# Reshaping the SBUF and DRAM transfers of a two-block attention kernel: relay of spare channels only, softmax sums by two SBUF transfers and a shuffle, output rows kept in place

## The chip, the cores and the metric

The kernel runs on one core of one Trainium2 chip. The metric is device time in microseconds (us), lower is better. All profiles are of one execution on that core. Most executions of one kernel agree within about 1%; an execution over 1.5% above the fastest of the same kernel is called slow.

## The reference, cut to what matters

Two independent attention blocks, A and B, work on 2048 tokens of width 640 (32 heads of 20 channels), in bf16. Their outputs stand side by side.

```python
def _A_ref(x, wqkv, wo):            # causal window of 256 tokens, softmax
    q, k, v = ...                   # x @ wqkv, 32 heads of 20
    scores = q k^T * 20**-0.5, masked to the window
    o = softmax(scores) v
    return o @ wo

def _B_ref(x, wqkv, wo):            # linear attention
    pq, pk = phi(q), phi(k)
    num = pq (pk^T v);  den = pq . sum(pk) + 1e-6
    return (num / den) @ wo
return concatenate([A, B], axis=-1)
```

The change touches block A alone, but both blocks share the engines.

## The kernel before

A planner inside the program orders all instructions at build time, from assumed durations; on the chip every engine then runs its own list strictly in order. SyncE ("SP") issues nearly all transfers, also in order.

Q and K of block A lie in tiles of 128 partitions: four heads ("a head group") of 32 rows each. A head has only 20 channels, so the last 12 rows of each of the first five tiles hold spare channels, from which the heads of tiles 5 to 7 are put together. That relay goes through DRAM. Attention weights times V give a tile ON per group (20 rows of values and one row of softmax sums per head); there are 16 groups, 8 for each half of the tokens.

```python
# relay of Q and K: all 128 rows out, then three tiles back (twice)
def relay_write(m, tt, key):
    dst = DQK[tt][0 : 32 * NH, :].rearrange("(r b) n -> b r n", b=NH)[4 * m : 4 * m + 4, :, :]
    dma("SP", ... q.dma_start(out=dst, in_=QK[m][:, c0 : c0 + RW]) ...)          # 4 x 32 x 2048
def relay_read(g, tt, key):
    src = bass.AP(..., ap=[[NH * RW, 4], [RW, 32], [1, RW]])                      # 4 x 32 x 2048
    dma("SP", ... q.dma_start(out=QK[g][:, c0 : c0 + RW], in_=src) ...)
# ... cut ...
# sums of one head group: four hops through DRAM, the last a broadcast of 512 KB
    dma("SP", ... out=d1[:], in_=ON[nb][Dh : Dh + 97 : 32, :] ...)                # 4 x 1024 f32
    dma("SP", ... out=RC[nb][:], in_=d1[:].rearrange("a (b c) -> (a b) c", c=32) ...)
    nc.vector.reciprocal(out=RD[nb][:], in_=RC[nb][:])
    dma("SP", ... out=d2[:].rearrange("a (b c) -> (a b) c", c=32), in_=RD[nb][:] ...)
    dma("SP", ... out=RB[nb][:], in_=d2[:, None, :].to_broadcast([4, 32, TQ]) ...)
    for rg in range(2):                                                            # normalise
        nc.vector.tensor_tensor(out=os_[:, c], in0=ON[nb][:, c], in1=RB[nb][:, c], op=ALU.mult)
    dma("SP", ... out=dst, in_=os_[:] ...)                                         # rows out, 256 KB
# ... cut ...
def o_read(tt, key, earliest=0.0):                                                 # rows back
    for m in range(KT):
        src = DO[tt][:].rearrange("(r b) n -> b r n", b=32)[4 * m : 4 * m + 4, :, :]
        dma("SP", ... out=OT[:, m, :], in_=src ...)                                # 256 KB
```

The softmax here doesn't subtract the row's maximum and nothing guards it: scores larger than these inputs give would overflow.

## Time and profile before

| | before |
|---|---|
| median of three runs | 470.98 us |
| span of the profiled execution | 470.0 us |
| busy: TensorE, VectorE, ScalarE, GpSimd | 305.6, 221.4, 191.5, 128.8 us |
| mean granted TensorE clock | 0.783 |
| moved by DMA | 50.32 MB |

The page of the kernel before. The first line gives each engine's busy time (PE is TensorE, DVE VectorE, ACT ScalarE, POOL GpSimd). The next lines cut the span into 40 slices, each digit the busy share in tenths; PEclk is the clock that TensorE was granted. Then come the bytes moved, and the chain of work that ended last, by line.

```profile
PE 305.6 (65%) x5000; PEld 166.6 (35%) x5000; DVE 221.4 (47%) x442; ACT 191.5 (41%) x168; POOL 128.8 (27%) x155
...
PE   5499964650577769559784759019576938859065
...
DVE  7155522540576652425442125028589776835024
...
PEclk9589977595697978779799766658858869988558
...
DMA packets 67756, 50.32 MB, mean 107 GB/s; under 512 B 52122, under 2 KB 58906, under 8 KB 67706
...
DMA RB<-d 22%; DMA RC<-d 8%; DMA d<-RD 8%; SPq L355 7%; DMA d<-ON 6%; PE F L657 3%; PE F L622 3%; PE F L424 3%; DVE OS L602 3%; DMA OT<-do 3%; DMA do<-OS 3%; PE F L394 3%; PE F L726 2%; PE SC L483 2%; PE F L572 2%
```

No engine is full. The digits of TensorE and VectorE often fall together, which suggests that one wait stops both. The four hops of the sums (RB<-d, RC<-d, d<-RD, d<-ON) are about 43% of the chain.

The list of waits on VectorE: what waited for what, us in total, how often, longest.

```profile
DVE OS L602 <- DMA RB<-d: 97.8, 13, 21.9
DVE RD L596 <- DMA RC<-d: 36.9, 9, 10.4
DVE G L317 <- PE F L622: 21.4, 10, 17.3
```

VectorE, in order, stood 134.7 us at the sums of softmax.

The table of stretches: busy us of each engine with instruction counts, granted clock, DMA share, GB/s.

```profile
110.00:120.00 10.00, 0.00 (x0) 0.00 (x0) 0.00 (x0) 0.00 (x0) 0.00 (x0) 0.50 0.94 97
```

In such a wait nothing runs at all, and the granted clock of TensorE is one half (0.50). The chain has d<-RD from 103.7 to 113.1 us there and RB<-d from 113.1 to 121.7.

The chain that ended last, in order of time (start, us, what): a piece of the middle, then the end.

```profile
171.41 1.81 DMA RC<-d
...
173.70 4.46 DMA d<-RD
...
178.17 12.93 DMA RB<-d
...
409.49 9.87 DMA d<-ON
...
438.57 13.16 DMA OT<-do
```

The broadcast RB<-d takes 8.0 us at best, in this chain up to 14.8. But d<-ON, which carries 16 KB, takes 9.9 us too. SyncE had issued a broadcast of 512 KB at 408.88 us, 0.6 us before this hop, and by the semaphore updates in the trace the two landed together, at 419.2 and 419.4 us. So the small transfer was queueing, not moving bytes.

SyncE's instructions in order of time (start, us, instruction) show the other side of the queue.

```profile
54.49 6.63 SPq L664 DMA_DIRECT2D XT<-in_B_x_dram  x2
```

The two issues of XT kept SyncE for 6.6 us.

### The profile page before, as it was taken

What the parts mean: (1) busy time and instruction counts of PE and PEld (TensorE: products, weight loads), DVE (VectorE), ACT (ScalarE), POOL (GpSimd) and SP (SyncE); (2) the same over time, 40 slices, a digit from 0 to 9 for tenths busy, and PEclk for the clock granted to TensorE, in tenths of its full rate; (3) what the DMA queues carried; (4) which work ended last, traced back from release to release, by engine and by line L of the source; (5) the groups of instructions that cost most, each with busy time, mean ns of one, the idle gap of its engine ahead of it and who ended that gap; (6) DMA issues with size and microseconds to landing.
All of it is one profiled execution on the core that took longest, in us unless ns stands there. A gap on an engine that the chain in (4) does not pass through costs nothing.

```text
span 470.0 us, 11365 instructions
## 1 busy us (share of the span) xinstructions
PE 305.6 (65%) x5000; PEld 166.6 (35%) x5000; DVE 221.4 (47%) x442; ACT 191.5 (41%) x168; POOL 128.8 (27%) x155
## 2 busy tenths in 40 slices
PE   5499964650577769559784759019576938859065
PEld 1155432330343325235352445004233415536033
DVE  7155522540576652425442125028589776835024
ACT  1058634370174835236363325107647737410000
POOL 9004313050043413113132013203335415312002
PEclk9589977595697978779799766658858869988558
DMA  5949999298694942143449999378413423333312
GB/s 115 241 100 80 136 108 101 70 109 100 88 106 104 108 86 91 46 139 103 131 139 112 96 89 183 118 78 90 62 60 99 131 90 115 123 116 146 118 59 96
DMA packets 67756, 50.32 MB, mean 107 GB/s; under 512 B 52122, under 2 KB 58906, under 8 KB 67706
## 3 DMA queue, kind: packets, MB, share of 16 engines
q1 hardware_dynamic: 60858, 40.97, 54.2%
q0 software_dynamic: 1600, 5.34, 2.9%
q10 hardware_dynamic: 5248, 3.28, 2.7%
q8 instruction: 39, 0.64, 0.8%
q14 instruction: 11, 0.09, 0.1%
HBM read 25.30 MB, written 16.52 MB: 89 GB/s over the span
## 4 chain that ended last, share of the span: by engine, by line
DMA 53%; PE 19%; DVE 12%; SPq 10%; issue 4%; ACT 1%; POOL 0%; POOLq 0%; DVEq 0%; ACTq 0%
DMA RB<-d 22%; DMA RC<-d 8%; DMA d<-RD 8%; SPq L355 7%; DMA d<-ON 6%; PE F L657 3%; PE F L622 3%; PE F L424 3%; DVE OS L602 3%; DMA OT<-do 3%; DMA do<-OS 3%; PE F L394 3%; PE F L726 2%; PE SC L483 2%; PE F L572 2%
## 5 line engine op out<-in xcount | busy, mean ns | idle before, releaser
L490 ACT ACTIVATE P<-SC 128x2048 bf16<-128x2048 f32 x78 | 146.4, 1877 | 144.9 <-PE SC L483 143.7
L513 POOL TENSOR_TENSOR P<-P,MK 128x512 bf16<-128x512 bf16 (+1 forms) x94 | 99.7, 1068 | 276.2 <-ACT P L490 272.0
L602 DVE TENSOR_TENSOR OS<-ON,RB 128x512 bf16<-128x512 f32 x32 | 23.2, 744 | 102.0 <-DMA RB<-d 97.8
L657 PE MATMUL F<-W,X 128*128 128x320 bf16 x160 | 30.5, 343 | 41.1 <-DVE R L317 36.8
L726 PE MATMUL F<-X,XT 128*128 128x512 bf16 x100 | 28.5, 424 | 27.4 <-DVE R L317 24.1
L572 PE MATMUL F<-P,V 64*32 64x64 bf16 (+4 forms) x2144 | 31.8, 254 | 21.2 <-issue 13.1
L622 PE MATMUL F<-W,OT 128*128 128x320 bf16 x160 | 30.1, 340 | 22.6 <-DMA OT<-do 16.0
L483 PE MATMUL SC<-QK 20*64 20x128 bf16 (+4 forms) x1600 | 36.6, 272 | 4.8 <-ACT P L490 3.1
L572 PEld LDWEIGHTS <-V 64*32 64x32 bf16 x2144 | 25.5, 101 | 33.8 <-issue 33.3
L657 PEld LDWEIGHTS <-X 128*128 128x128 bf16 x160 | 16.2, 108 | 52.5 <-issue 44.1
L317 DVE CAST R<-F 128x320 bf16<-128x320 f32 (+1 forms) x55 | 28.2, 521 | 13.1 <-PE F L622 5.6
L394 PE MATMUL F<-X,WK 128*128 128x512 bf16 x75 | 25.0, 466 | 8.1 <-DVE G L317 4.8
L317 DVE CAST QK<-F 128x512 bf16<-128x512 f32 x31 | 21.1, 683 | 18.5 <-PE F L394 18.3
L394 PE MATMUL F<-X,WQ 128*128 128x512 bf16 x75 | 23.3, 429 | 9.9 <-DVE V L317 4.1
L483 PEld LDWEIGHTS <-QK 20*64 20x64 bf16 x1600 | 16.2, 111 | 36.0 <-issue 35.0
L317 DVE CAST G<-F 128x320 bf16<-128x320 f32 (+2 forms) x34 | 16.2, 486 | 26.7 <-PE F L622 21.4
L622 PEld LDWEIGHTS <-OT 128*128 128x128 bf16 x160 | 16.6, 107 | 32.8 <-DMA OT<-do 17.7
L666 PE MATMUL F<-R,XT 128*128 128x320 bf16 x160 | 27.2, 321 | 1.6 <-DVE ON L317 1.6
L513 DVE TENSOR_TENSOR P<-P,MK 128x512 bf16<-128x512 bf16 (+1 forms) x54 | 25.7, 482 | 3.7 <-ACT P L490 3.4
L424 PE MATMUL F<-WV,X 128*128 128x320 bf16 x120 | 23.8, 358 | 5.6 <-DMA WV<-in_A_wqkv_dram 4.1
L648 ACT ACTIVATE E<-R 128x640 bf16<-128x640 bf16 (+1 forms) x26 | 17.4, 688 | 20.2 <-DVE R L317 20.2
L726 PEld LDWEIGHTS <-XT 128*128 128x128 bf16 x100 | 11.4, 123 | 39.9 <-issue 33.1
(85 smaller groups left out, 339.9 us busy)
## 6 DMA issues: line engine op xcount, KB each, us to landing
RB<-d SPq DMA_DIRECT2D x16, 512.0 KB
dqk<-QK SPq DMA_DIRECT2D x10, 512.0 KB
do<-OS SPq DMA_DIRECT2D x16, 256.0 KB
QK<-dqk SPq DMA_DIRECT2D x6, 512.0 KB
XT<-in_B_x_dram SPq DMA_DIRECT2D x5, 512.0 KB
OT<-do SPq DMA_DIRECT2D x10, 256.0 KB
out_dram<-ST POOLq DMA_DIRECT2D x12, 160.0 KB, 2.7
out_dram<-G POOLq DMA_DIRECT2D x10, 160.0 KB, 2.9
```

The source lines that it names most:

```text
L317: nc.vector.tensor_copy(out=dst, in_=src)
L355: q.dma_start_transpose(out=X[slot][:, c, :], in_=xsrc[which][t * NX : (t + 1) * NX, c, :])
L394: mms.append((mm_t(NX), xkey(slot, k) + [("wqk", i, 0 if m == 0 else 1)], lambda ps, k=k: nc.tensor.matmul(ps[:], lhsT=WQK[i][:, k, m * P ...
L424: mms = [(mm_t(HALF), xkey(slot, k) + [("wv",)], lambda ps, k=k, hf=hf: nc.tensor.matmul(ps[:, 0:HALF], lhsT=X[slot][:, k, (kb % 4) * P : ...
L483: nc.tensor.matmul(SC[64 * rho : 64 * rho + 64, j, cc : cc + w], lhsT=QK[g][32 * j : 32 * j + Dh, kc : kc + 64], rhs=QK[g][32 * j : 32 * j ...
L490: nc.scalar.activation(out=pt[:], in_=SC[:], func=ACT.Exp, scale=scale)
L513: eng.tensor_tensor(out=pt[:, :, cc : cc + w], in0=pt[:, :, cc : cc + w], in1=MK[:, None, lo:hi].to_broadcast([P, 4, w]), op=ALU.mult)
L572: nc.tensor.matmul(FB[box[rg]][32 * j : 32 * j + 32, qc : qc + w], lhsT=V[kb % NV][64 * rho : 64 * rho + 64, HV * h : HV * h + 32], rhs=PT ...
L602: pl.op({"DVE": dve_ps(NX)}, lambda e, c=c: nc.vector.tensor_tensor(out=os_[:, c], in0=ON[nb][:, c], in1=RB[nb][:, c], op=ALU.mult), -2900 ...
L622: mms = [(mm_t(HALF), [lkeys(c)] if not isinstance(lkeys(c), list) else lkeys(c), lambda ps, c=c, hf=hf: nc.tensor.matmul(ps[:, 0:HALF], l ...
L657: mms = [(mm_t(HALF), [("x", slot, k), ("w1",)], lambda ps, k=k, b=b, hf=hf: nc.tensor.matmul(ps[:, 0:HALF], lhsT=X[slot][:, k, b * P : (b ...
L726: mms = [(mm_t(NX), [("x", slot, k)] + XK, lambda ps, k=k, c=c: nc.tensor.matmul(ps[:], lhsT=XW[:, k, :].rearrange("p (f c) -> p c f", c=K ...
```

## The change

The intent is that the large transfers run on 12 to 16 DMA engines and not on few. Four things change, and two assumed latencies of the planner.

1. Relay: only the 12 spare rows of a head are written, one transfer per head; the reads become one plain 128-row transfer.
2. Sums: two SBUF-to-SBUF hops of 16 KB. The second leaves one row of reciprocals in each group of 32 partitions, and a VectorE shuffle spreads it over the 32.
3. Rows: groups 0 to 4 are normalised straight into their final tile; only groups 5 to 7 go through DRAM, and they are read back into the spare rows of the five final tiles.
4. Order: groups 5 to 7 come before 3 and 4, so that the last reads are few.

```diff
+    GO = [[0, 1, 2, 5, 6, 7, 3, 4], [0, 1, 2, 5, 6, 7, 3, 4]]
-    def dma(eng, fn, mb, key, r=(), w=(), lat=2.2, ...
+    def dma(eng, fn, mb, key, r=(), w=(), lat=2.8, ...
     # relay
-        dst = DQK[tt][0 : 32 * NH, :].rearrange("(r b) n -> b r n", b=NH)[4 * m : 4 * m + 4, :, :]
-        dma("SP", lambda q: q.dma_start(out=dst, in_=QK[m][:, c0 : c0 + RW]), ...)
+        for j in range(4):
+            dma("SP", lambda q, j=j: q.dma_start(out=DQK[:, 4 * m + j, :], in_=QK[m][32 * j + Dh : 32 * j + 32, c0 : c0 + RW]), ...)
-        src = bass.AP(tensor=b.tensor, offset=b.offset, ap=[[NH * RW, 4], [RW, 32], [1, RW]])
+        src = DQK[4 * (g - KT) : 4 * (g - KT) + 4, :, :].rearrange("i d n -> (i d) n")
     # sums
-        (four transfers through d1 and d2)
+        dma("SP", lambda q: q.dma_start(out=RC[nb][:], in_=ON[nb][Dh : Dh + 97 : 32, :]), ...)
         reciprocal RD <- RC
+        dma("SP", lambda q: q.dma_start(out=RB[0:97:32, :], in_=RD[nb][:]), ...)
+            nc.vector.stream_shuffle(out=RB[:, c], in_=RB[:, c], mask=[0] * 32)
     # rows
+        if g >= KT: dst = OS        # spare groups, through DRAM
+        elif tt == 0: dst = OT[:, g, :]
+        else: dst = QK[g][:, 0:TQ]
     # ... cut: o_read in three pieces of 12-row transfers, RB set to 1.0 once ...
```

More of the change, by code (lines that the diff above doesn't have):

```diff
@@ L259 @@
     ON = [T([P, TQ], f"ON{i}", F32) for i in range(2)]
-    RB = [T([P, TQ], "RB", F32)] * 2
+    RB = T([P, TQ], "RB", F32)
     OT = T([P, KT, TQ], "OT")
-    OS = [T([P, TQ], f"OS{i}") for i in range(2)]
+    OS = T([P, TQ], "OS")
     ST = [T([P, D], f"ST{i}") for i in range(2)]
@@ L292 @@
         nc.gpsimd.memset(V[i][:], 1.0)
+    nc.gpsimd.memset(RB[:], 1.0)
     nc.gpsimd.memset(blk4[:], 1.0)
@@ L306, in qe, with dma @@
         return nc.sync if e == "SP" else nc.scalar if e == "ACTQ" else nc.gpsimd
-    def dma(eng, fn, mb, key, r=(), w=(), lat=2.2, n=1, earliest=0.0, tag=""):
+    def dma(eng, fn, mb, key, r=(), w=(), lat=2.8, n=1, earliest=0.0, tag=""):
         return pl.op({eng: (1.0 if eng == "POOL" else 0.6) * n}, lambda e: fn(qe(e)), key, r, w, lat=lat + 5.0 * mb, earliest=earliest, tag=tag)
@@ L355, in fn @@
                 q.dma_start_transpose(out=X[slot][:, c, :], in_=xsrc[which][t * NX : (t + 1) * NX, c, :])
-            pl.op({"SP": 1.3}, lambda e, fn=fn: fn(nc.sync), key, (), xkey(slot, c), lat=2.2, earliest=earliest, tag=f"x{which}{t}")
+            pl.op({"SP": 1.3}, lambda e, fn=fn: fn(nc.sync), key, (), xkey(slot, c), lat=3.0, earliest=earliest, tag=f"x{which}{t}")
     def wview(w):
@@ L400, with relay_tail @@
     RW = 4 * NX
-    DQK = [dram.tile([33 * NH, RW], BF16, name=f"dqk{i}") for i in range(2)]
-    def relay_tail(tt, key):
-        src = bass.AP(tensor=A_x.tensor, offset=A_x.offset, ap=[[RW, 12], [1, RW]])
-        dma("POOL", lambda q: q.dma_start(out=DQK[tt][32 * NH : 32 * NH + 12, :], in_=src), 0.1, key, w=[("dqk", tt)], tag="tail")
+    DQK = dram.tile([LEFT, 32, RW], BF16, name="dqk")
+    def relay_tail(key, earliest):
+        src = bass.AP(tensor=A_x.tensor, offset=A_x.offset, ap=[[LEFT * RW, LEFT], [1, LEFT * RW]])
+        dma("SP", lambda q: q.dma_start(out=DQK[:, Dh:32, :], in_=src), 0.6, key, w=[("dqkt",)], earliest=earliest, tag="tail")
     def relay_write(m, tt, key):
@@ L409, in relay_write @@
         cols = range(0, 4) if tt else range(1, 5)
-        dst = DQK[tt][0 : 32 * NH, :].rearrange("(r b) n -> b r n", b=NH)[4 * m : 4 * m + 4, :, :]
-        dma("SP", lambda q: q.dma_start(out=dst, in_=QK[m][:, c0 : c0 + RW]), 0.52, key, r=[("QK", m, z) for z in cols], w=[("dqk", tt)], tag=f"rlw{m}")
+        for j in range(4):
+            dma("SP", lambda q, j=j: q.dma_start(out=DQK[:, 4 * m + j, :], in_=QK[m][32 * j + Dh : 32 * j + 32, c0 : c0 + RW]), 0.05, key, r=[("QK", m, z) for z in cols], w=[("dqk",)], tag=f"rlw{m}")
     def relay_read(g, tt, key):
@@ L415, in relay_read @@
         cols = range(0, 4) if tt else range(1, 5)
-        o = (Dh + 4 * (g - KT)) * NH
-        b = DQK[tt][o : o + 92, :]
-        src = bass.AP(tensor=b.tensor, offset=b.offset, ap=[[NH * RW, 4], [RW, 32], [1, RW]])
-        dma("SP", lambda q: q.dma_start(out=QK[g][:, c0 : c0 + RW], in_=src), 0.52, key, r=[("dqk", tt)], w=[("QK", g, z) for z in cols], tag=f"rlr{g}")
+        src = DQK[4 * (g - KT) : 4 * (g - KT) + 4, :, :].rearrange("i d n -> (i d) n")
+        dma("SP", lambda q: q.dma_start(out=QK[g][:, c0 : c0 + RW], in_=src), 0.52, key, r=[("dqk",), ("dqkt",)], w=[("QK", g, z) for z in cols], tag=f"rlr{g}")
     def proj_v(kb, slot, key, earliest=0.0, step=0.05):
@@ L434 @@
     for tt in range(2):
-        for g in range(8):
+        for g in GO[tt]:
             for kb in (range(0, 8) if tt == 0 else range(6, 16)):
@@ L517 @@
     npv = [0]
-    DO = [dram.tile([32 * 32, TQ], BF16, name=f"do{i}") for i in range(2)]
+    DO = dram.tile([LEFT, 32, TQ], BF16, name="do")
     def pv_group(tt, g):
@@ L590, in pv_group @@
         ev.give = True
-        d1 = dram.tile([4, TQ], F32, name=f"d1_{tt}_{g}")
-        d2 = dram.tile([4, TQ], F32, name=f"d2_{tt}_{g}")
         kk = -4000
-        dma("SP", lambda q: q.dma_start(out=d1[:], in_=ON[nb][Dh : Dh + 97 : 32, :]), 0.02, kk, [("on", nb)], [("d1", tt, g)], tag="den1")
-        dma("SP", lambda q: q.dma_start(out=RC[nb][:], in_=d1[:].rearrange("a (b c) -> (a b) c", c=32)), 0.02, kk, [("d1", tt, g)], [("rc", nb)], tag="den2")
+        dma("SP", lambda q: q.dma_start(out=RC[nb][:], in_=ON[nb][Dh : Dh + 97 : 32, :]), 0.05, kk, [("on", nb)], [("rc", nb)], tag="den1")
@@ L596, in pv_group @@
         pl.op({"DVE": 0.35}, lambda e: nc.vector.reciprocal(out=RD[nb][:], in_=RC[nb][:]), -3200, [("rc", nb)], [("rd", nb)], tag="recip")
-        dma("SP", lambda q: q.dma_start(out=d2[:].rearrange("a (b c) -> (a b) c", c=32), in_=RD[nb][:]), 0.02, kk, [("rd", nb)], [("d2", tt, g)], tag="den3")
-        dma("SP", lambda q: q.dma_start(out=RB[nb][:], in_=d2[:, None, :].to_broadcast([4, 32, TQ])), 0.3, kk, [("d2", tt, g)], [("rb",)], lat=2.6, tag="den4")
-        os_ = OS[nb]
+        dma("SP", lambda q: q.dma_start(out=RB[0:97:32, :], in_=RD[nb][:]), 0.05, kk, [("rd", nb)], [("rb0",)], tag="den2")
@@ L600, in pv_group @@
+        if g >= KT:
+            dst, dk = OS[:], [("os",)]
+        elif tt == 0:
+            dst, dk = OT[:, g, :], [("on1", tt, g)]
+        else:
+            dst, dk = QK[g][:, 0:TQ], [("on1", tt, g), ("QK", g, 0), ("QK", g, 1)]
         for rg in range(2):
             c = slice(rg * NX, (rg + 1) * NX)
-            pl.op({"DVE": dve_ps(NX)}, lambda e, c=c: nc.vector.tensor_tensor(out=os_[:, c], in0=ON[nb][:, c], in1=RB[nb][:, c], op=ALU.mult), -2900, [("on", nb), ("rb",)], [("os", nb)], tag="norm")
@@ L603, in pv_group @@
-        if g < KT:
-            dst = DO[tt][:].rearrange("(r b) n -> b r n", b=32)[4 * g : 4 * g + 4, :, :]
-        else:
-            o = 32 * (Dh + 4 * (g - KT))
-            dst = DO[tt][o : o + P, :]
-        dma("SP", lambda q: q.dma_start(out=dst, in_=os_[:]), 0.26, kk, [("os", nb)], [("do", tt)], tag="ow")
-    def o_read(tt, key, earliest=0.0):
-        for m in range(KT):
-            src = DO[tt][:].rearrange("(r b) n -> b r n", b=32)[4 * m : 4 * m + 4, :, :]
-            dma("SP", lambda q, m=m, src=src: q.dma_start(out=OT[:, m, :], in_=src), 0.26, key, [("do", tt)], [("ot", m)], earliest=earliest, tag="or")
+            pl.op({"DVE": 0.62}, lambda e, c=c: nc.vector.stream_shuffle(out=RB[:, c], in_=RB[:, c], mask=[0] * 32), -2900, [("rb0",)], [("rb", rg)], tag="shuf")
@@ new lines, in pv_group, with o_read @@
+            pl.op({"DVE": dve_ps(NX)}, lambda e, c=c: nc.vector.tensor_tensor(out=dst[:, c], in0=ON[nb][:, c], in1=RB[:, c], op=ALU.mult), -2900, [("on", nb), ("rb0",), ("rb", rg)], dk, tag="norm")
+        if g >= KT:
+            src = DO[4 * (g - KT) : 4 * (g - KT) + 4, :, :].rearrange("i d n -> (i d) n")
+            dma("SP", lambda q: q.dma_start(out=src, in_=OS[:]), 0.26, kk, [("os",)], [("do",)], tag="ow")
+    def o_read(tt, m0, m1, key):
+        for q_ in range(4):
+            if tt == 0:
+                src = DO[:, 4 * m0 : 4 * m1, :].rearrange("i (m q) n -> i m q n", q=4)[:, :, q_, :]
+                dma("SP", lambda q, q_=q_, src=src: q.dma_start(out=OT[32 * q_ + Dh : 32 * q_ + 32, m0:m1, :], in_=src), 0.05 * (m1 - m0), key, [("do",)] + [("on1", tt, m) for m in range(m0, m1)], [("ot", tt, m) for m in range(m0, m1)], tag="or")
+                continue
+            for m in range(m0, m1):
+                dma("SP", lambda q, q_=q_, m=m: q.dma_start(out=QK[m][32 * q_ + Dh : 32 * q_ + 32, 0:TQ], in_=DO[:, 4 * m + q_, :]), 0.05, key, [("do",), ("on1", tt, m)], [("ot", tt, m)], tag="or")
@@ L639, in a_out @@
         for b in range(8):
-            finish_rows(tt * 8 + b, 0, lambda c, b=b: OT[:, c, b * P : (b + 1) * P], lambda c: [("ot", c)], lambda c, hf: WOA[:, c, hf * HALF : (hf + 1) * HALF], [("w1",)], key + 0.1 * b, earliest)
+            finish_rows(tt * 8 + b, 0, lambda c, b=b: (QK[c] if tt else OT[:, c, :])[:, b * P : (b + 1) * P], lambda c: [("ot", tt, c)], lambda c, hf: WOA[:, c, hf * HALF : (hf + 1) * HALF], [("w1",)], key + 0.1 * b, earliest)
     ne = [0]
@@ L778 @@
                 proj_qk(i, m, t, 3 * t, (4 if m == 1 else 17 + 4 * m) + 2 * t + i)
-    for tt in range(2):
-        relay_tail(tt, 0)
+    relay_tail(-3000, 24.0)
     for m in range(KT):
@@ L786 @@
     u = 0
-    for g in range(8):
+    for g in GO[0]:
         while u <= last_unit[(0, g)]:
@@ L791 @@
         pv_group(0, g)
-    assert u == last_unit[(0, 7)] + 1
+    assert u == last_unit[(0, GO[0][-1])] + 1
     b_keys(0, 1, 50)
@@ L820 @@
     load_woa(-90, 60.0)
-    o_read(0, -3500)
+    for m0, m1 in ((0, 3), (3, 4), (4, 5)):
+        o_read(0, m0, m1, -3500)
     a_out(0, 210, 0.0)
@@ L831 @@
     b_kvwo(158)
-    for g in range(8):
+    for g in GO[1]:
         while u <= last_unit[(1, g)]:
@@ L843 @@
         b_query(t, slot, 140 + 8 * t, 200 + 5 * t)
-    o_read(1, -3500)
+    for m0, m1 in ((0, 3), (3, 4), (4, 5)):
+        o_read(1, m0, m1, -3500)
     a_out(1, 300)
```

## The prediction

> **What bounds the kernel now.** No engine is full: the busy table gives TensorE 305.6 us of 470.0 (65%), VectorE 221.4, ScalarE 191.5, GpSimd 128.8. The chain of work that ended last is 53% DMA, and most of that is the softmax-denominator relay of 16 head groups: RB<-d 22%, RC<-d 8%, d<-RD 8%, d<-ON 6%. The waits list shows the mechanism: VectorE, which runs in order, stood 97.8 us (13 times, longest 21.9) at the normalising multiply for RB and 36.9 us at the reciprocal for RC, 134.7 us together. TensorE, ScalarE and GpSimd stop with it, since VectorE empties most PSUM banks (windows 110-120 and 300-310 us have no engine busy). The tail is serial too: in the chain's last 65 us (405 to 470) the last group costs d<-ON 9.9, RC<-d 1.8, d<-RD 1.4, RB<-d 9.5, two normalises, do<-OS 2.0, OT<-do 13.2, then the output matmuls.
>
> **Why it is slow.** RB<-d moves 512 KB and never took less than about 8.0 us in the chain: 65 GB/s, where early slices show 220 to 241. The Trainium skill ("DMA: Bandwidth & Descriptors", section "Why a DMA increments its semaphore by 16 and not by 1") says the slowest dimension sets how many engines share a transfer. Here it is 4 for RB<-d, dqk<-QK and OT<-do; 65 GB/s agrees with four engines. The other relays queue behind them: d<-ON, 16 KB, takes 1.5 to 10 us.
>
> **What changes.**
> - Removed: per group, two of four DMA hops and the 512 KB broadcast (8 MB in all); 10 of 16 row writes (2.5 MB); most of the relays, since only 12 of 32 channels per head go (5 MB to 1.9 MB of writes, on 12 engines).
> - Added: 32 shuffles on VectorE. One 128x512 f32 multiply here takes 0.69 us; I estimate 0.6 us each, 20 us of VectorE. SyncE gets more, smaller issues of about 0.55 us (relay writes 10 to 40, row reads 10 to 32) against 42 fewer.
> - Moved: groups 5-7 come before 3 and 4, so at the end only two short reads remain; the schedule is also rebuilt with longer assumed DMA latencies.
>
> **Costs.** Estimated from RC<-d 1.75 and d<-RD 1.42: the two new hops, probably on 4 engines but only 16 KB, take 2 to 3.5 us each. Per group the relay falls from about 14 to 25 us to 7 to 9, some two to four VectorE instructions of which the new order covers. VectorE's denominator waits of 134.7 us should fall to about 40. OT<-do at the end falls from 13.2 to 3 to 4 us. Against this: shuffles +20 us busy, mostly visible because VectorE is near-critical after 320 us, and loss of fill. TensorE's clock falls to 0.50 in the dead windows (mean 0.783), so fewer stops also shorten its 305.6 us, by my estimate 15.
>
> 470 - 95 (waits) - 10 (tail) - 15 (clock) + 20 (shuffles) + 8 (SyncE queueing, partial overlap) = 378 us.
>
> **Predicted: 378 us, range 348 to 412. Faster by over 2%: 0.93; within 2%: 0.04; slower: 0.03.**
>
> **Right if:** RB and RC waits on VectorE sum under 60 us; RB's transfers land within 4 us; no window of 10 us without work after startup; DMA share of the chain falls below 35%; mean TensorE clock rises above 0.83; shuffles take 0.55 to 0.7 us.
>
> **Wrong if:** the DMA transposes of x hold SyncE's in-order queue (one blocked it 8.3 us at 95 us), so that even short hops wait behind them; the 4-partition destination is slow; moving groups 5-7 forward makes scores wait for the first relay; VectorE, near 240 us busy, becomes the bound. Better than predicted if the stalls vanish altogether: then TensorE's shortened busy time sets about 340.

## The result, and the profile after

The changed kernel took 324.54 us (median of four, 321.88 to 327.34, the last of them counted as slow) against 471.97 us of before. The ratio is 0.686, interval 0.679 to 0.694. A ratio here is the mean time of one kernel's fast runs over that of the other's of the same rounds, so not quite the ratio of the medians.

The prediction, 378 us with 348 to 412, had the direction right. It was 54 us too high: the measured time lies below its whole range.

The page after:

```profile
PE 264.1 (82%) x4969; PEld 154.5 (48%) x5000; DVE 242.0 (76%) x495; ACT 197.9 (62%) x183; POOL 127.9 (40%) x150
...
PE   5257999979988878999989998986868687979593
...
DVE  7515565679998888658668268999999999987553
...
PEclk9559999979999999999999979999999899999978
...
DMA packets 63028, 34.63 MB, mean 108 GB/s; under 512 B 52406, under 2 KB 59190, under 8 KB 62966
...
PE F L396 6%; PE F L424 6%; DMA RB<-RD 5%; PE F L660 5%; DVE RB L603 4%; DVE E L652 4%; PE F L669 4%; PE F L625 4%; DVE R L653 4%; ACT P L490 4%; SPq L357 4%; DVE P L513 3%; PE SC L483 3%; DVE ON L319 3%; DVE OT L604 3%
```

The holes are gone. No line has more than 6% of the chain, and VectorE is at nine tenths or more for most of the time from 200 to 285 us. The waits on VectorE after; for RC there is none in the list:

```profile
DVE G L319 <- PE F L625: 6.3, 10, 3.5
DVE RB L603 <- DMA RB<-RD: 6.1, 4, 2.3
```

The same stretch as shown of before, and the chain piece of one hop:

```profile
110.00:120.00 10.00, 7.60 (x163) 4.13 (x160) 8.41 (x19) 7.69 (x7) 5.18 (x5) 1.00 0.43 80
```

```profile
106.32 3.07 DMA RB<-RD
...
109.42 1.37 DVE RB L603 x3
```

SyncE in order of time: the same two XT issues, and the transfers of the last head group.

```profile
55.62 2.47 SPq L667 DMA_DIRECT2D XT<-in_B_x_dram  x2
...
289.31 0.55 SPq L592 DMA_DIRECT2D RC<-ON  x1
...
293.22 0.55 SPq L594 DMA_DIRECT2D RB<-RD  x1
300.18 1.51 SPq L616 DMA_DIRECT2D QK<-do  x4
```

The XT issues now keep SyncE for 2.5 us instead of 6.6. These transfers were not edited.

Where the time went can be written down exactly from VectorE's side, because a span is busy time plus idle time:

| VectorE, us | before | after | difference |
|---|---|---|---|
| busy | 221.4 | 242.0 | +20.6 |
| idle, waiting for RB or RC | 134.7 | 6.1 | -128.6 |
| idle, everything else (span less the two above) | 113.9 | 72.4 | -41.5 |
| span | 470.0 | 320.5 | -149.5 |

TensorE gives the same sum in another way: its busy time fell by 41.5 us (305.6 to 264.1) and its idle time by 108.0 us (164.4 to 56.4). The work is the same 5000 weight loads and matmuls (a few matmul records are missing after); its mean clock rose from 0.783 to 0.948. That the two engines both show 41.5 is chance.

### The profile page after: what moved, and what is told of

It reads as the page before. It is cut to its first block, busy times and chain, and to the rows that moved or that the text cites. A ratio compares the mean times of both kernels' runs of the same rounds, so it can differ in the third digit from the quotient of the medians.

```text
span 320.5 us, 11419 instructions
## 1 busy us (share of the span) xinstructions
PE 264.1 (82%) x4969; PEld 154.5 (48%) x5000; DVE 242.0 (76%) x495; ACT 197.9 (62%) x183; POOL 127.9 (40%) x150
## 4 chain that ended last, share of the span: by engine, by line
DVE 39%; PE 30%; DMA 9%; issue 9%; SPq 6%; ACT 4%; POOL 2%; POOLq 0%; DVEq 0%; ACTq 0%
PE F L396 6%; PE F L424 6%; DMA RB<-RD 5%; PE F L660 5%; DVE RB L603 4%; DVE E L652 4%; PE F L669 4%; PE F L625 4%; DVE R L653 4%; ACT P L490 4%; SPq L357 4%; DVE P L513 3%; PE SC L483 3%; DVE ON L319 3%; DVE OT L604 3%
## 5 line engine op out<-in xcount | busy, mean ns | idle before, releaser
L660 PE MATMUL F<-W,X 128*128 128x320 bf16 x160 | 25.7, 313 | 4.8 <-DVE R L319 2.5
L729 PE MATMUL F<-X,XT 128*128 128x512 bf16 x94 | 23.9, 381 | 6.7 <-DVE G L319 1.5
L483 PEld LDWEIGHTS <-QK 20*64 20x64 bf16 x1600 | 15.6, 104 | 27.1 <-issue 25.9
L319 DVE CAST R<-F 128x320 bf16<-128x320 f32 (+1 forms) x43 | 22.0, 518 | 8.5 <-PE F L625 4.6
L572 PE MATMUL F<-P,V 64*32 64x64 bf16 (+4 forms) x2144 | 27.3, 226 | 0.9 <-issue 0.8
L424 PE MATMUL F<-WV,X 128*128 128x320 bf16 x120 | 20.0, 314 | 7.1 <-DMA WV<-in_A_wqkv_dram 3.3
L653 DVE SCALAR_TENSOR_TENSOR R<-R,E 128x640 bf16<-128x640 bf16 (+1 forms) x26 | 24.0, 930 | 0.1
L396 PE MATMUL F<-X,WK 128*128 128x512 bf16 x63 | 19.0, 399 | 5.1 <-DVE WK L319 3.2
L603 DVE STREAM_SHUFFLE RB<-RB 128x512 f32<-128x512 f32 x32 | 22.1, 729 | 0.0
L660 PEld LDWEIGHTS <-X 128*128 128x128 bf16 x160 | 15.7, 102 | 12.7 <-issue 5.6
L319 DVE CAST V<-F 128x320 bf16<-128x320 f32 x25 | 12.0, 489 | 10.3 <-PE F L424 10.1
L424 PEld LDWEIGHTS <-X 128*128 128x128 bf16 x120 | 11.8, 102 | 14.6 <-issue 8.9
```

The costliest lines, as they stand in the source:

```text
L319: nc.vector.tensor_copy(out=dst, in_=src)
L396: mms.append((mm_t(NX), xkey(slot, k) + [("wqk", i, 0 if m == 0 else 1)], lambda ps, k=k: nc.tensor.matmul(ps[:], lhsT=WQK[i][:, k, m * P ...
L424: mms = [(mm_t(HALF), xkey(slot, k) + [("wv",)], lambda ps, k=k, hf=hf: nc.tensor.matmul(ps[:, 0:HALF], lhsT=X[slot][:, k, (kb % 4) * P : ...
L483: nc.tensor.matmul(SC[64 * rho : 64 * rho + 64, j, cc : cc + w], lhsT=QK[g][32 * j : 32 * j + Dh, kc : kc + 64], rhs=QK[g][32 * j : 32 * j ...
L572: nc.tensor.matmul(FB[box[rg]][32 * j : 32 * j + 32, qc : qc + w], lhsT=V[kb % NV][64 * rho : 64 * rho + 64, HV * h : HV * h + 32], rhs=PT ...
L603: pl.op({"DVE": 0.62}, lambda e, c=c: nc.vector.stream_shuffle(out=RB[:, c], in_=RB[:, c], mask=[0] * 32), -2900, [("rb0",)], [("rb", rg)] ...
```

## The experiments

Two theories stood after the result. Theory A: the chain of the sums, with its 512 KB broadcast, stalled VectorE; the rest is decoration. Rival B: transfers confined to few DMA engines, the Q/K relay and the rows among them, hold up everything that is issued behind them, so the reshaping of transfers that nobody waits for is part of the gain. In all, 18 runs were made, repeats among them. All results were correct except one, noted below. Each was run beside the kernel before. Where the text gives a saving for c1 or c3b, or a loss between a2 and b4, it is worked out from the fast runs alone; the medians in the table are over all runs.

| run | what it is | median us | ratio to before | interval |
|---|---|---|---|---|
| changed | the change | 324.54 | 0.686 | 0.679 to 0.694 |
| a1_sums_only | before + new sums | 420.69 | 0.895 | 0.891 to 0.899 |
| c1_relay_only | before + new relay | 420.84 | 0.886 | 0.877 to 0.895 |
| c3b_rows_and_order_old | change, old rows and order | 352.02 | 0.741 | 0.734 to 0.748 |
| a2_sums_old | change, old sums | 389.63 | 0.827 | 0.822 to 0.832 |
| c2_relay_old | change, old relay | 398.02 | 0.844 | 0.836 to 0.852 |
| a3_wide_broadcast | before, broadcast in 4 pieces | 432.88 | 0.921 | 0.916 to 0.927 |
| d2_relay_wide | before, relay in pieces | 425.75 | 0.907 | 0.900 to 0.915 |
| d1_all_wide | before, all large ones in pieces | 369.62 | 0.786 | 0.780 to 0.791 |
| b4_four_hops_wide | a2, broadcast in 4 pieces | 343.84 | 0.731 | 0.726 to 0.735 |

### One part alone: the sums, the relay

`a1_sums_only`: the kernel before with the part "sums" of the diff above, nothing else.

> The kernel before with only the new path of the sums (two SBUF-to-SBUF hops of 16 KB and the VectorE shuffle); relay of Q and K, output rows, group order and assumed latencies as before. Theory A (the denominator chain with its 512 KB broadcast is what stalled VectorE): 335 to 370 us, VectorE waits for RB and RC together fall from 134.7 us to under 40 us. Rival B (the other transfers that run on few engines, the Q/K relay and the rows, hold up even short hops, so all three reshapings are needed): 400 us or more, with over 60 us of waits for RC and RB left.

Measured: 420.69 us, ratio 0.895. Theory A is refuted as stated, and B's side of the expectation holds. The waits of VectorE:

```profile
DVE RB L599 <- DMA RB<-RD: 47.7, 8, 10.8
DVE RD L594 <- DMA RC<-ON: 45.0, 7, 15.3
```

These are the same two hops of 16 KB that cost 6.1 us of waiting in the changed kernel; here they cost 92.7 us. SyncE's instructions in order of time show what they meet:

```profile
56.00 0.56 SPq L593 DMA_DIRECT2D RC<-ON  x1
56.62 8.19 SPq L662 DMA_DIRECT2D XT<-in_B_x_dram  x2
64.90 1.74 SPq L412 DMA_DIRECT2D dqk<-QK  x1
66.75 0.55 SPq L595 DMA_DIRECT2D RB<-RD  x1
67.39 10.36 SPq L356 DMA_TRANSPOSE X<-in_B_x_dram  x4
```

The hop RC<-ON is issued at 56.0 us and lands at 64.9: the chain shows it for 8.90 us. For nearly all of that time SyncE is held by two other issues, until 64.8. One of the relay's old 512 KB writes, issued at 53.3 us, is still going out: by the semaphore updates in the trace it lands at 64.6, just before the hop.

`c1_relay_only`: the kernel before with the part "relay" alone.

> The kernel before with only the Q/K relay changed: 12 spare channels per head written as four transfers on 12 engines, reads of 512 KB on 16. Sums alone gave 0.895, so theory A (sums are the main thing) leaves this at 450 to 470 us. Rival B (transfers on few engines block every hop behind them): 420 to 445 us, with VectorE waits for RC falling from 37 us to under 20 us while those for RB stay over 70 us.

Measured: ratio 0.886, some 54 us. The two fast runs (415.88 and 418.35 us) lie even below B's range. In d2 below, which widens the same relay, RB waits were 69.2 us and RC waits 22.8 us, against 97.8 and 36.9 before. In the waits of before no computing engine waits for this relay at all, and yet it is worth as much as the part with all the waiting. Its time was not priced in the prediction at all.

### One part undone

`a2_sums_old` is the changed kernel with the four hops and the one-piece broadcast put back and the shuffle taken out. `c2_relay_old` is the changed kernel with the old relay.

> The changed kernel with the old path of the sums put back (four hops through DRAM, broadcast of 512 KB as one transfer, no shuffle). Theory A: 400 to 450 us, VectorE waits for RB and RC over 80 us. Rival B: under 365 us, because the other transfers no longer stand in the way.

> The changed kernel with the old Q/K relay put back (full 128 rows, 512 KB, on few engines). Rival B: the 16 KB hops of the sums wait behind the relay again, VectorE waits for RC and RB grow from 6 us to over 25 us, time 340 to 370 us. Theory A: within 3% of the changed kernel, under 335 us.

Measured: 389.63 us for a2, between the two expectations, with RB and RC waits of 71.2 us (A asked for over 80). For c2, 398.02 us, beyond what B expected; its waits on VectorE:

```profile
DVE RB L605 <- DMA RB<-RD: 34.6, 5, 20.0
DVE RD L595 <- DMA RC<-ON: 26.5, 6, 6.9
```

So with either half put back alone, 61 to 71 us of waiting for the sums are there again. Alone the sums give 49 us and the relay 54. Together, in c3b, they give some 122 us (ratio 0.741), with 21.2 us of RB and RC waits left. c3b also has the new planner latencies; a4 below shows that these are worth nothing in the changed kernel. The parts help each other, which a sum of separate terms cannot show.

### The same bytes on more engines

The Trainium skill, page "DMA: Bandwidth & Descriptors", section "Why a DMA increments its semaphore by 16 and not by 1", states that a transfer uses as many engines as the largest number up to 16 that divides the slowest dimensions of both sides. An access of 4 x 32 x 2048 would use four. The page of the profile does not show which engine moved what, so the rule was tested by time: the same bytes, in the same plan, with an outer dimension of 32.

The trace kept with each run can be asked more closely than its page, and it agrees with the rule. It records every semaphore update that comes from a DMA. Counted per transfer, up to the next issue on the same semaphore, nearly all with an outer dimension of 4 (dqk<-QK, QK<-dqk, RB<-d, OT<-do and d<-ON of before) have 5 updates, the 12-row relay writes of the changed kernel have 13, and those with an outer dimension of 32 or 128 have 16. I read this as one for each engine, and one more where fewer than 16 take part.

The kernel before also holds a test within itself, without any cutting into pieces: its row writes do<-OS are all single transfers of 256 KB. The ten with an outer dimension of 4 took 5.7 to 15.3 us to land, the six with 128 rows 2.0 to 6.1. (Their rows also lie differently in DRAM, and the load around them differs.) This speaks against the rival that the smaller pieces alone help; no run cut a transfer into pieces without widening it.

`a3_wide_broadcast` and `d1_all_wide` (the latter does the like for relay writes and reads, row writes and row reads; `d2_relay_wide` for the relay alone):

```diff
-        dma("SP", lambda q: q.dma_start(out=RB[nb][:], in_=d2[:, None, :].to_broadcast([4, 32, TQ])), ...)
+        def bc4(q):
+            for j in range(4):
+                q.dma_start(out=RB[nb][32 * j : 32 * j + 32, :], in_=d2[j : j + 1, :].to_broadcast([32, TQ]))
+        dma("SP", bc4, ...)
```

> The kernel before, same order on every engine, with only the 512 KB broadcast issued as four transfers of 32 rows each, whose slowest dimension is 32 instead of 4. If the number of engines sets its duration, the broadcast lands in 3 to 4 us instead of 8 or more and the kernel takes 390 to 435 us; the three short hops still wait. If the bytes, not the engines, set it, it lands in about 8 us still and the time stays within 2% of before (or worse, with three more issues of 0.55 us per group).

> The kernel before, same plan and same bytes, with every transfer that had an outer dimension of 4 or less and over 16 KB issued as four transfers with an outer dimension of 32 (broadcast, relay writes and reads, row writes and reads); the four hops stay. The broadcast alone so gave 0.921. If the number of engines is what the change is about, this alone takes most of the gain: 345 to 385 us. If the cut in bytes and hops counts as much, 395 to 425 us; with some 200 more transfer issues on SyncE it may lose part of what it wins.

> The kernel before, same plan, same bytes, only the Q/K relay's writes and reads issued as four transfers of 32 rows. The relay with 12 spare channels on 12 engines gave 0.886. If the engines are what counts, the same here: 410 to 425 us. If the bytes count, clearly less gain: 440 to 460 us.

Measured: 0.921 for a3, inside the first expectation of time; all four pieces of a broadcast landed within 3.9 us at best and 4.9 us in the median, against some 8.0 and 9.0 us in one piece. But its RC waits grew from 36.9 to 45.0 us; I take it that the other transfers still stood in the way. d2 took 425.75 us, just outside its first range of 410 to 425. Its 0.907 is near c1's 0.886 though it cuts no bytes: for the relay the engines are most of it, the bytes probably the rest (the two were in different rounds). And d1 took 369.62 us, 0.786. It moves the same bytes as before, in the page's words:

```profile
DMA packets 70877, 50.34 MB, mean 137 GB/s; under 512 B 55242, under 2 KB 62026, under 8 KB 70826
```

With the same four hops, the same bytes and the order of before, 100.5 of the change's 147.4 us are there, and RB and RC waits are down from 134.7 to 55.0 us. A page of instructions in order shows SyncE freed in d1, at the two XT issues and the hop after them:

```profile
55.11 2.25 SPq L687 DMA_DIRECT2D XT<-in_B_x_dram  x2
57.47 1.72 SPq L603 DMA_DIRECT2D RC<-d  x1
```

These two issues took 6.63 us in before, 8.19 in a1 and 10.01 in c2, all with the old relay; they took 2.25 in d1, 1.93 in d2 and 2.47 in the changed kernel, all with a relay of many engines. The DMA transposes of x show the same. Their SyncE durations (min/median/max ns, first and last start), of before, then of d1, then of the changed kernel:

```profile
L355 SPq DMA_TRANSPOSE X<-in_B_x_dram x40: 1122/1674/8593, 13.8 to 326.2; - x40
```

```profile
L355 SPq DMA_TRANSPOSE X<-in_B_x_dram x40: 1121/1211/2637, 13.8 to 251.6; - x40
```

```profile
L357 SPq DMA_TRANSPOSE X<-in_B_x_dram x40: 1122/1212/2496, 13.8 to 206.6; - x40
```

So there are two delays, and more engines remove both. A hop issued behind a backlog lands late, and SyncE, blocked on its next issue, cannot issue the following hop at all. That the block is a full queue on the loaded engines is an inference; the profile shows the duration and what removes it, not the queue.

`b4_four_hops_wide`: a2 with the broadcast in four pieces, the same plan.

> a2_sums_old (389.6 us) with the same plan, its 512 KB broadcast issued as four transfers of 32 rows; four hops, no shuffle. If the number of engines is the cause, it takes most of the 66 us that a2 lost: 325 to 350 us, RB waits from 63 us to under 25 us. If hops or bytes are, 365 to 385 us.

Measured: 343.84 us, as the first expectation; RB waits fell from 63.0 to 27.1 us (under 25 were expected). Of the some 66 us between a2 and the changed kernel, about 45 were the width of one transfer (a2, b4 and the changed kernel are of different rounds, so these are differences of the ratios 0.827, 0.731 and 0.686). The remaining 21 us or so are the hops, the bytes and the different plan together; they were not taken apart further.

### What the prediction had added or left out: latencies, rows, order, shuffle

`a4_old_latency` is the changed kernel with 2.2 us assumed for transfers and transposes.

> The changed kernel planned with the old assumed DMA latencies (2.2 us instead of 2.8, transposes 2.2 instead of 3.0). If the vanished waits owe much to a plan that places the waiting VectorE instructions later, VectorE waits for RB and RC grow from 6 us to 20 us or more and the time is 332 to 350 us. If the short hops alone do it, within 2% of the changed kernel.

Measured: 322.65 us, 0.682 (0.678 to 0.685). No effect. Waits for RC and RB were 11.4 us instead of 6.1. The plan is not why the waits vanished.

`c3_rows_old` put the old row path into the changed kernel but kept the new order.

> The changed kernel with the old output rows put back (all 16 groups written to DRAM, ten reads of 256 KB), new group order kept. The last read of about 13 us returns to the end of the chain, so at least 10 us more: 335 to 345 us if that is all; 345 to 370 us if the row traffic also delays the hops of the sums (rival B), then with waits for RC and RB over 20 us.

Its result was wrong, by a mistake in the experiment: the old writes of groups 0 to 4 carry rubbish in the spare rows, which the later groups 5 to 7 used to overwrite, and the new order turned that round. It took 356.11 us. `c3b_rows_and_order_old` mends it with the old order:

> c3_rows_old gave a wrong result because the old row writes of groups 0 to 4 carry rubbish in the spare rows and the new order puts groups 3 and 4 after the spare groups; here the old order goes with the old rows, so the result is right. Expected as for c3: about 356 us by the measured c3, 345 to 370 us.

Measured: 352.02 us. The next run differs from it only in the rows:

> The changed kernel with only the group order put back (0 to 7). If the order is worth something, the last groups' row reads return to the end: 12 short reads of some 0.4 us each and one group more after the relay, 327 to 335 us. If not, within 1% of the changed kernel.

`b3_old_order` took 318.89 us, ratio 0.678 (0.674 to 0.681), faster than the changed kernel and against both halves of the expectation. Rows in place are thus worth 30 us in the same rounds (fast runs of c3b and b3), and the new order nothing. Repeats with five rounds:

> The changed kernel itself, as the control of these rounds: 320 to 327 us, ratio about 0.686.

> The changed kernel with the old group order once more, five rounds: ratio 0.678 as measured first, against 0.695 of the changed kernel in the last rounds, so 315 to 321 us. If the two were only apart by chip and rounds, the ratio comes out at 0.69 to 0.695.

The changed kernel gave 0.695 (0.692 to 0.698), the old order 0.676 (0.672 to 0.680). They were not in the same rounds, but both beside before. In the repeats the intervals stand apart; in the first pair they just overlap (0.679 to 0.694 and 0.674 to 0.681). So the new order gains nothing and seems to cost 1 to 3%. Why was not found out.

`f1_shuffle_twice` does each shuffle twice, in the same place.

```diff
-            lambda e, c=c: nc.vector.stream_shuffle(out=RB[:, c], in_=RB[:, c], mask=[0] * 32)
+            lambda e, c=c: [nc.vector.stream_shuffle(out=RB[:, c], in_=RB[:, c], mask=[0] * 32) for _ in range(2)]
```

> The changed kernel with every VectorE shuffle done twice, so 32 more of 0.73 us, 23 us of VectorE, in the same order. The prediction added 20 us for the shuffles as if all of it were visible. If so, 340 us or more, 20 us above the changed kernel of these rounds. If most of it falls into VectorE's idle time (78 us of 320), 5 to 12 us above it.

Measured: 344.79 us, 17.7 us above the changed kernel's 327.10 of the same rounds. The added work is 32 times 0.73 us, 23.4 us; some three quarters of it show. The instructions of the shuffle line in the changed kernel (min/median/max ns):

```profile
L603 DVE STREAM_SHUFFLE RB<-RB x32: 715/727/764, 62.1 to 298.2; 128x512 f32<-128x512 f32 x32
```

The term of 20 us was about right.

### Can both be beaten?

`g1_three_hops_no_shuffle` takes the shuffle away for one hop more and the wide broadcast, in the old order.

> Old group order; sums by one SBUF hop, one hop to DRAM and a broadcast of 512 KB in four transfers of 32 rows; no shuffle. If VectorE is what bounds the changed kernel after 200 us, its 22 us fewer win: 308 to 318 us. If the longer chain (one hop and some 1.7 us of issues more) and the 8 MB bring waits back, 322 to 335 us.

Measured: 340.79 us, 0.725, worse even than expected of the bad case. RB and RC waits came to 20.3 us. That alone does not make 21 us against the old-order run, since the shuffles were saved; the rest is open.

`g2_last_stores_sp` takes the old order and issues the last eight stores of block A from SyncE. `h1_faster_pace` was meant to change the plan's spacing on top.

> Old group order; the last eight stores of the window-attention rows issued by SyncE instead of GpSimd, whose issues come 1.36 us apart at the end. If those issues bound the end, 2 to 4 us less than the old-order run (318.9 us): 314 to 318 us. If the output matmuls and evacuations bound it, within 1 us of it.

> Old order, last stores on SyncE (0.674), and the plan's spacing of score units cut from 2.62 to 2.45 us. If the spacing holds work back, 308 to 314 us. If VectorE and TensorE, busy 76% and 86%, bound it, within 1% of 317.7 us.

g2 took 317.71 us, 0.674 (0.671 to 0.677), 3% under the changed kernel of the same rounds (327.10). Against the old order alone (0.678 and 0.676) it can't be told apart. h1 turned out to build the very same instruction order as g2 on all five engines, so it says nothing of the spacing. It is a repeat: 317.61 us, 0.673. The old group order, with or without the stores, is the version that beats both kernels.

## Why the prediction was right or wrong

The accounting of VectorE's span puts numbers on the terms of its sum. Only the rows together are exact: that the last three terms of the prediction belong to the other idle time is how I sorted them.

| term of the prediction | predicted | measured | verdict |
|---|---|---|---|
| waits for RB and RC, 134.7 to about 40 us | -95 | -128.6 (6.1 left) | mis-sized by 34 |
| shuffles | +20 | +20.6 VectorE busy, 22.1 of shuffle | right |
| tail, clock and SyncE queueing (-10, -15, +8) | -17 | -41.5 other idle time of VectorE | mis-sized by 25 |
| sum | -92 | -149.5 | 57 short |

The first term failed, at its overlap. The prediction said that waits "should fall to about 40": a relay of 7 to 9 us per group, made of hops of 2 to 3.5 us, "some two to four VectorE instructions of which the new order covers". The times were right. Counted in the trace of the changed kernel, each hop took about 2 us in the median, and from the issue of the first to the landing of the second it was 7.6 us (median of the 16 groups; 5.7 to 12.5). The cover was wrong: between that first issue and the shuffle, VectorE ran 13 other instructions, 7.4 us of work (medians, without the reciprocal). So 6.1 us of waiting were left. It is not the new order that covers: with the old order (b3) it was 14.5 instructions, and 9.2 us of waits.

The reading behind the term also had a gap. It priced the sums as a chain of its own, with hop times taken from uncongested cases, and gave the Q/K relay no term; the times came out only because the relay was reshaped too. It had itself written that "the other relays queue behind them". The runs show that a hop's time is not its own. The same two hops cost 92.7 us of waiting with everything else as before (a1), 61.1 us with only the relay as before (c2), and 6.1 us with all of it reshaped. The relay alone is worth 54 us and its removal from the change costs 71 us or more (398.02 against 324.54 and 327.10).

The term for SyncE most likely had the wrong sign. "More, smaller issues" were to cost 8 us. In fact all its transfer instructions together took 236.0 us before (202 of them) and 156.8 us after (213), by a sum over the traces, for long ones fell away: the median transpose of block B went from 1.67 to 1.21 us, the longest from 8.6 to 2.5. d1 issues even more transfers (358) and gains 100 us. What this is worth in the span was not measured apart.

The clock term had the right mechanism and too small a size. TensorE's busy time fell by 41.5 us, not 15. The Trainium skill, page "TensorE: Matmul & The Clock Gate", section "What's actually happening", states that the clock is halved when TensorE has been idle and comes back after sustained work. The trace agrees: 0.50 in the dead stretch 110 to 120 us of before, 1.00 in the same stretch after. Shorter waits thus pay twice. This is not an extra saving on top of the table above, only the same span seen from TensorE. How much of the 41.5 us lay on the critical path is not shown.

The tail was underrated. From the last weights-times-V matmul to the end it took 63.4 us before (406.6 to 470.0) and 32.7 us after (287.8 to 320.5). The prediction's 10 us counted only the row read there; the hops of the last group, which fell too, are part of its first term. VectorE's waits for the output matmuls in this stretch (G<-F in the lists above) fell from 21.4 to 5.7 us.

Right were the direction, the engines as the cause of slow transfers (d1, b4 and the counts of updates), the times of the new hops, the cost of the shuffles, and four of its six signs: waits under 60 us (6.1), no dead stretch of 10 us, DMA share of the chain under 35% (9%), mean clock above 0.83 (0.948). Two were not quite: one RB<-RD of the chain took 6.5 us, above the 4 us, and the shuffle took 0.73 us, just above its 0.55 to 0.70. Wrong was that the new order is a gain.

## What to carry to other kernels

When a small transfer takes as long as a large one, price the queue, not the transfer: look for what was issued before it, even if no engine waits for that. Make the outer dimension of every large transfer a multiple of 16 first; in this kernel that alone, with the same bytes, gave two thirds of the gain. Waits on an in-order engine do not add up term by term: two parts worth 49 and 54 us alone were worth some 122 us together.

## What the Trainium skill lacked or had wrong

- "DMA: Bandwidth & Descriptors", section "Rules for kernel authors", advises to coalesce small transfers into one large one, and not to bother with two transfers to disjoint partition halves. The second assumes that both halves already run on all 16 engines. Where the large one has an outer dimension of 4, the opposite held: four transfers of 32 rows in place of one of 128 took the kernel from 470.15 to 369.62 us (d1) and from 389.63 to 343.84 us (b4). The same table's row on using all 16 engines agrees with the runs; the rows should name each other.
- Apart from a part on DMA between cores, no passage that I found on that page tells that SyncE's issue itself is held up by a backlog. Two plain issues took 6.63 us with the relay on few engines and 1.93 us with the same bytes on more (before and d2); one DMA transpose held SyncE for 8.6 us (before) and none over 2.7 us with all transfers wide (d1).
- "VectorE: DVE Perf Modes", section "The perf-mode tier table", gives about 2400 ns for a shuffle of 2048 elements. It has no figure for other lengths, and the time is not in proportion: that would be 600 ns for 512, where the trace has 727 ns.
- No page that I found has the latency of an SBUF-to-SBUF hop that gathers four rows into 128 partitions (RC<-ON). Here 16 KB took 2.0 to 2.3 us from issue to landing in the changed kernel, by the semaphore updates of its trace, and 8.9 us behind the old relay (a1).
